# An attention and MLP kernel: the order of the first loads, 21 idle matmuls, and where a weight's high halves are computed

## The chip, the core and the metric

One core of a Trainium2 chip (trn2). The metric is device time of one execution in microseconds (us), as the median of several runs. The engines are TensorE (PE; its weight loads are shown as PEld), VectorE (DVE), ScalarE (ACT), GpSimd (POOL) and SyncE (SP), which issues all DMAs of this kernel.

## What is computed

`x` is 1 x 2048 x 512 in float32. Two branches read the layer-normed `x`; one is a sliding, dilated attention with 32 heads of 16 values, the other an MLP with 1376 hidden units that layer-norms once more.

```python
xn = _layernorm(x, axis=-1)
s = _A_ref(xn, A_wqkv, A_wo)     # q,k,v = xn @ wqkv; each row sees 8 rows, 2 apart, backwards; softmax; @ wo
g = _silu(_B_ref(xn, B_w1, B_b1, B_w2, B_b2))   # gelu(layernorm(xn) @ w1 + b1) @ w2 + b2
return x + s * g
```

## The kernel before

Rows of `x` are split by parity (`c` = 0, 1; the attention goes in steps of two rows) and then into 8 tiles of 128 rows. For a parity the layer-normed tiles are transposed on the PE into `yT`, 512 columns each, and kept there.

**Two halves for each number.** Matmuls run in float16, but every operand is held as a scaled high half and a low half that holds the rest, and each product is made of three: high x high, high x low, low x high. So each weight (`wqkv` in four blocks `hb`, `w1`, `w2`, `wo`) goes through the same steps after its load: ACT sums its squares (`sumsq`, and `prep_q` for `wqkv`), a matmul with the constant tile `fours` adds the sums up over the partitions (`total`, on the PE), a few DVE operations on one column make a power of two from it (`half_exp`, `up`, `down`), then ACT writes the high half (`split`, or `hi` in `prep_q`) and DVE the low half (`lo`, a scalar_tensor_tensor that reads the weight and its high half). `w2` has 11 blocks `k`: the first 8 lie in `yT` tiles, the last 3 in tiles `f`.

**Opening.** `LOADS` sets the order of the first DMAs: `q0` (the first block of `wqkv`, in two parts), then tiles 2 and 3 of `x`, then the other tiles in pairs. `ln0` handles a group of tiles: `stats` (bn_stats and bn_aggr on DVE), `factors` (power -1/2 on POOL, a few DVE columns), the normed tile on DVE or, for the tiles in `ACT_Y`, on ACT (`y_act`), four PE transposes, the high half by ACT, the low half by DVE. `qkv(c, hb, u)` then makes q, k and v of a tile with 12 matmuls of 384 columns, in the order of `IORD`, and ACT writes them to `U`.

**The rest.** `attention` runs on DVE with some additions on POOL. `mlp1(ch, f)` makes 128 hidden units of 512 rows: 12 matmuls of 512 columns, then on ACT the gelu, the high half, and for the first 8 blocks a low half that starts with one more matmul with the diagonal tile `dg`. `mlp2` adds the block into four PSUM tiles. `wo_first` and `wo_last` multiply by `wo`, and DVE and POOL finish the output.

**What sets the order.** All operations are recorded in a plan (`Plan`) with an engine, an estimated duration, what they read and write, and a priority. `Plan.issue` places them one by one: of the operations that could start next on an engine, the one with the smallest priority value within a small window. The program's order on each engine is the result, and each engine then runs its own queue in that order, waiting on semaphores. DMAs are issued by SP in the order of the plan. An operation marked `port` shares a lock in the plan with all others so marked, on DVE and POOL.

## Time and profile before

| | |
|---|---|
| time, median of 3 runs | 425.15 us (423.82 to 425.76) |
| the profiled execution | 426.52 us, its span 424.7 us |
| mean granted TensorE clock | 0.992 |
| busy in the span | PE 406.7 us (96%), DVE 396.7 (93%), ACT 217.6 (51%), POOL 97.8 (23%) |
| costliest group | 768 projection matmuls (L545), 129.3 us busy |
| DMA | 44.83 MB, 106 GB/s on average |

The span runs from the first to the last instruction of the program; the time of an execution has some 1.8 us around it. In the rows of the timeline the columns are the start in us, the duration in us, the engine, the source line and operation, output<-inputs by tile names, the shape, how many instructions were merged, and in brackets how long the engine had been idle and what ended that.

### The profile page before, as it was taken

To read this page: it belongs to the slowest core of one execution; us is meant where nothing else is said; L and a number is where in the kernel's file an instruction comes from. 1 tells how busy PE (TensorE), PEld (TensorE's weight loads), DVE (VectorE), ACT (ScalarE), POOL (GpSimd) and SP (SyncE) were. 2 spreads that over 40 slices of the span, in tenths; PEclk is the share of its full clock that TensorE was granted. 3 is DMA by queue.
4 is the path that set the end of the run, shared out by engine and by line. 5 is a ranking of instruction groups with operands and counts; after the bars stand their busy time and mean duration, and the time that the engine had idled before them with its cause. 6 is when DMAs were issued, how large, how long until landed. Compare 5 with 4: busy or idle time off the path is not lost.

```text
span 424.7 us, 5503 instructions
## 1 busy us (share of the span) xinstructions
PE 406.7 (96%) x2072; PEld 206.6 (49%) x2072; DVE 396.7 (93%) x434; ACT 217.6 (51%) x340; POOL 97.8 (23%) x87
## 2 busy tenths in 40 slices
PE   0999979999999999999999999999999999999995
PEld 0666524445544654445544654455445544444442
DVE  3998999998999979999999999998999999999966
ACT  4799975845376456744466254125312284226400
POOL 5310202002500382002700360046002610250013
PEclk9999969999999999999999999999999999999999
DMA  8964420003241235742162034022423264005325
GB/s 277 412 245 148 146 79 0 2 7 143 85 101 50 100 87 120 129 109 43 54 180 100 0 88 99 2 74 80 155 98 107 69 161 174 0 2 127 122 49 198
DMA packets 43050, 44.83 MB, mean 106 GB/s; under 512 B 27496, under 2 KB 28064, under 8 KB 42768
## 3 DMA queue, kind: packets, MB, share of 16 engines
q1 hardware_dynamic: 43024, 44.49, 34.7%
q8 instruction: 16, 0.26, 0.3%
q14 instruction: 10, 0.08, 0.1%
HBM read 23.53 MB, written 7.34 MB: 73 GB/s over the span
## 4 chain that ended last, share of the span: by engine, by line
PE 84%; ACT 9%; DVE 3%; DMA 2%; issue 1%; SPq 0%; DVEq 0%
PE z L826 27%; PE mh L785 26%; PE ps L545 22%; PE ps L723 6%; ACT w L376 2%; ACT U L553 2%; DMA prod<-in_A_x_dram 2%; ACT w L339 1%; PE z L723 1%; PE mh L723 1%; DVE U L714 1%; DVE U L767 1%; ACT wq L402 1%; ACT yT L495 1%; DVE bn L458 1%
## 5 line engine op out<-in xcount | busy, mean ns | idle before, releaser
L545 PE MATMUL ps<-wq,yT 128*128 128x384 f16 x768 | 129.3, 328 | 0.0
L785 PE MATMUL mh<-yT,w 128*128 128x512 f16 (+1 forms) x528 | 123.5, 385 | 0.9 <-ACT h L813 0.9
L826 PE MATMUL z<-w,h 128*128 128x512 f16 x480 | 112.0, 379 | 0.0
L545 PEld LDWEIGHTS <-yT 128*128 128x128 f16 x768 | 75.5, 99 | 51.1 <-issue 1.5
L785 PEld LDWEIGHTS <-w 128*128 128x128 f16 (+1 forms) x528 | 53.4, 101 | 65.8 <-issue 6.3
L798 ACT ACTIVATE mh<-mh,b1T,hsc 128x512 f32<-128x512 f32 (+1 forms) x44 | 33.0, 749 | 88.0 <-PE mh L785 87.8
L596 DVE TENSOR_TENSOR prod<-U 128x2048 f32<-128x2048 f32 x32 | 74.1, 2317 | 1.0
L826 PEld LDWEIGHTS <-h 128*128 128x128 f16 x480 | 47.1, 98 | 55.3 <-issue 0.3
L599 DVE TENSOR_REDUCE L<-prod 128x128 f32<-128x2048 f32 x32 | 72.9, 2279 | 0.3
L553 ACT ACTIVATE U<-ps,cs 128x384 f32<-128x384 f32 x64 | 37.2, 581 | 67.4 <-PE ps L545 63.4
L653 DVE TENSOR_TENSOR prod<-L,U 128x2048 f32<-128x2048 f32 x28 | 63.4, 2285 | 0.1
L676 POOL COPY gate<-prod 1x1 f32<-1x1 f32 x21 | 4.4, 208 | 210.7 <-DVE prod L596 204.2
L648 DVE TENSOR_TENSOR prod<-prod,prod 128x2048 f32<-128x2048 f32 x16 | 36.5, 2284 | 0.0
L677 POOL TENSOR_TENSOR prod<-prod 128x1024 f32<-128x1024 f32 x14 | 32.9, 2347 | 0.0
L723 PEld LDWEIGHTS <-oT 128*128 128x128 f16 x192 | 18.8, 98 | 22.4
L801 ACT ACTIVATE h<-mh,hsc 128x512 f16<-128x512 f32 x40 | 27.4, 685 | 0.9
L723 PE MATMUL ps<-wo,oT 128*128 128x512 f16 x120 | 26.9, 379 | 0.0
L804 DVE SCALAR_TENSOR_TENSOR h<-mh,hsc,h 128x512 f16<-128x512 f32 x32 | 23.8, 744 | 2.8 <-ACT h L801 2.8
L607 POOL TENSOR_TENSOR L<-L,misc 1x384 f32<-1x384 f32 x8 | 19.4, 2430 | 20.6 <-DVE L L599 20.6
L677 POOL TENSOR_TENSOR prod<-prod,prod 128x1024 f32<-128x1024 f32 x7 | 16.4, 2344 | 0.0
L798 ACT ACT_TABLE_LOAD x12 | 15.4, 1283 | 0.2
L636 ACT ACTIVATE o<-prod,osc 128x1024 f16<-128x1024 f32 (+1 forms) x9 | 9.4, 1050 | 11.5 <-DVE prod L648 6.2
(144 smaller groups left out, 338.1 us busy)
## 6 DMA issues: line engine op xcount, KB each, us to landing
f<-in_A_x_dram SPq DMA_DIRECT2D x31, 256.0 KB, 3.7
U<-U SPq DMA_DIRECT2D x16, 392.0 KB, 3.7
gd<-f SPq DMA_DIRECT2D x12, 256.0 KB, 2.0
oT<-in_B_w_dram SPq DMA_DIRECT2D x2, 1024.0 KB
yT<-in_B_w_dram SPq DMA_DIRECT2D x2, 1024.0 KB
f<-gd SPq DMA_DIRECT2D x8, 256.0 KB, 3.4
out_dram<-f SPq DMA_DIRECT2D x8, 256.0 KB, 2.0
out_dram<-U SPq DMA_DIRECT2D x8, 256.0 KB, 2.3
```

The lines of the kernel that those rows point to most:

```text
L545: nc.tensor.matmul(b.t[:, 0:384], y[:, s, k, o:o + P], wq[:, hb, k, t], start=(n == 0), stop=(n == 11))
L553: act(384, lambda i=i, b=b: nc.scalar.activation(U3[:, i:i + 31:15, :], b.t[:, 0:384].rearrange("p (t e) -> p t e", t=3), AF.Identity, sca ...
L596: dve(2048, lambda p2=p2, g=g: nc.vector.tensor_tensor(p2(), q, slots(Ut, KH, 2 * g), op=ALU.mult), qk + [("kh", ub, 0), ("kh", ub, 1), (" ...
L599: dve(2048, lambda pr=pr, g=g: nc.vector.tensor_reduce(L3()[:, 2 * g:2 * g + 2], pr.t.rearrange("p (r f d) -> p r f d", r=2, d=DH), AX.X, ...
L648: dve(n, lambda: nc.vector.tensor_tensor(d(), a(), b(), op=ALU.add), keys, [dkey])
L653: dve(2048, lambda: nc.vector.tensor_tensor(pr.t.rearrange("p (r f d) -> p r f d", r=2, d=DH), L3()[:, 2 * g:2 * g + 2].rearrange("p r (f ...
L677: nc.gpsimd.tensor_tensor(x.t[:, 0:1024], x.t[:, 0:1024], y(), op=ALU.add)
L723: nc.tensor.matmul(b.t, oT[:, hb, i // 4, s, i % 4], wo[:, hb, t], start=(hb == 0 and n == 0), stop=(hb == NHB - 1 and n == 2))
L785: nc.tensor.matmul(b.t[0:M], w1[:, k, s, f * P:f * P + M], yT[ch][:, t, k], start=(n == 0), stop=(n == 11))
L798: act(512, lambda: nc.scalar.activation(b.t[0:M], b.t[0:M], AF.Gelu_apprx_tanh, bias=b1T[0:M, f:f + 1], scale=hsc[0:M, 1:2]), [b, ("b1T",) ...
L801: act(512, lambda: nc.scalar.activation(hi()[0:M], b.t[0:M], AF.Identity, scale=hsc[0:M, 2:3]), [b], [hk])
L826: nc.tensor.matmul(z.t, hl[s][0:K, t * P:(t + 1) * P], w2[0:K, f, w], start=(f == 0 and n == 0), stop=(f == NF - 1 and n == 2))
```

## The change

The core of the diff (planner constants and the lines that only split a matmul group into smaller pieces are cut):

```diff
-LOADS = ["q0", (2, 1), (3, 1), (0, 2), (4, 2), (6, 2)]
+LOADS = [(2, 1), (3, 1), "q0", "q2", (0, 2), (4, 2), (6, 2)]
...
-                    t, o = min((x for x in lst if x[0] <= t0 + WINDOW), key=lambda x: (x[1].prio, x[1].n))
+                    t, o = min((x for x in lst if x[0] <= t0 + (WINDOW if x[1].prio > PURG else WURG)),
+                               key=lambda x: (x[1].prio, x[1].n))
...
+WAKE = 21
+QHI = 4
...
     def total(dst, dkey, cols, n, ckeys, late=False):
...
+        if n == 2:
+            for k in range(2):
+                pl.add("pe", 0.15, lambda k=k: nc.tensor.matmul(
+                    b.t[:, 0:1], fours, cols()[:, k:k + 1], start=(k == 0), stop=(k == 1)),
+                    [ckeys[k]], [b], prio=min(pl.prio, PTOT))
+            n = 1
...
+    def on_pool(n, hi, src, s, r, w, **k):
+        pool(0.3 + n * POOL1, lambda: nc.gpsimd.tensor_scalar(hi, src(), s, 1.0, op0=ALU.mult, op1=ALU.mult),
+             r, [w], port=False, **k)
...
-    def split(hi, lo, src, s, r, w):
+    def split(hi, lo, src, s, r, w, eng="act"):
...
+        if eng == "pool":
+            on_pool(n, hi, get, s, r, (w, "hi"))
+        else:
+            act(n, lambda: nc.scalar.activation(hi, get(), AF.Identity, scale=s), r, [(w, "hi")])
...
-    IORD = [2, 3, 1, 4, 5, 6, 7, 0]
+    IORD, IORD0 = [2, 3, 1, 4, 5, 6, 7, 0], [2, 3, 0, 1, 4, 5, 6, 7]
...
-            for n0 in range(0, 12, 4) if u < 2 else (0,):
-                n1 = n0 + 4 if u < 2 else 12
+            ends = [1, 2, 3, 4, 8, 12] if u == 0 and i == IORD0[0] else [4, 8, 12] if u < 2 else [12]
+            for n0, n1 in zip([0] + ends, ends):
...
+    idle = fours.bitcast(BF16)
+    for _ in range(WAKE):
+        b = R_mh.new()
+        pl.add("pe", 0.2, lambda b=b: nc.tensor.matmul(b.t[:, 0:2 * P], idle[:, 0:P], idle, start=True,
+                                                       stop=True), [("yd", 2)], [b], prio=1e9)
...
-        sumsq(lambda k=k: cw1.t[:, k:k + 1], (cw1, k), s1a[:, k], ("s1a", k),
+        sumsq(lambda k=k: cw1.t[:, k:k + 1], (cw1, k), s1a[:, k], [("s1a", k)] + [("y_", i) for i in BEFORE_W1],
...
             split(w2[:, k, 0], w2[:, k, 1], (s2a, s2b)[k // 4][:, k % 4], zsc[:, 0:1],
-                  [("s2", k // 4), ("zsc0",), ("w2j", k // 4), ("yT", 2 + k // 4)], ("w2", k))
+                  [("s2", k // 4), ("zsc0",), ("w2j", k // 4), ("yT", 2 + k // 4)], ("w2", k),
+                  "act" if k < 2 else "pool")
         else:
             b = s2c[k - 8]
-            act(512, lambda k=k, K=K, b=b: nc.scalar.activation(
-                w2[0:K, k, 0], b.t[0:K], AF.Identity, scale=zsc[0:K, 0:1]),
-                [b, ("zsc0",), ("w2j", k)], [("w2h", k)])
+            on_pool(512, w2[0:K, k, 0], lambda b=b, K=K: b.t[0:K], zsc[0:K, 0:1],
+                    [b, ("zsc0",), ("w2j", k)], ("w2h", k))
...
+    warm = sb.tile([1, 1], F32, name="warm")
+    act(1, lambda: nc.scalar.activation(warm, ident[0:1, 0:1], AF.Gelu_apprx_tanh),
+        [("y", 0, i) for i in range(NI)] + [("wq", 1, k) for k in range(KT)], [("warm",)], table="gelu")
```

In words: tiles 2 and 3 of `x` are loaded ahead of `q0`; the sum of squares of a `wqkv` block is added up by two matmuls, one for each part, instead of one; the bias column is no longer made for the tiles that DVE norms; ACT's squares of `w1` come after its normed tiles; 21 matmuls of 256 columns on the constant tile `fours`, whose results nobody reads, stand in the PE's queue; nine of the eleven high halves of `w2` (blocks 2 to 10) are written by POOL; an activation on one element loads ACT's gelu table earlier; and the planner weighs priorities in a smaller window, so that the order of the opening changes. `QHI` is 4 and there are four parts, so its branch is never taken.

The first rows of the PE's queue, from the first transposes to the first projections, before (`f_102` and `f_103` are normed tiles, `z` PSUM tiles for transposes and sums, `ps` the projections, `s_128` the columns of sums of the first block of `wqkv`):

```order
L345 MATMUL z_153<-s_128,fours 128x2
L491 MATMUL z_156<-ident,f_102 128x128 x4
L491 MATMUL z_154<-ident,f_103 128x128 x4
L545 LDWEIGHTS yT_88
L545 MATMUL ps_149<-wq,yT_88 128x384
```

And now (`mh_151` and `mh_152` are the PSUM tiles that the idle matmuls write):

```order
L531 MATMUL z_156<-ident,f_102 128x128 x4
L965 LDWEIGHTS fours
L965 MATMUL mh_151<-fours 128x256
L965 LDWEIGHTS fours
L965 MATMUL mh_152<-fours 128x256
L965 LDWEIGHTS fours
L965 MATMUL mh_151<-fours 128x256
L362 MATMUL z_153<-s_128,fours 128x1
```

In one piece, the sums' matmul moves behind the first transposes and three idle matmuls. After these rows come four more idle matmuls, the transposes of the second tile, the second matmul on the sums, fourteen more idle matmuls, and then the projections: everything behind an idle matmul waits for it.

The stretch of ACT's queue that leads to the first gelu, before (`w_85` is `w1` and `w_86` is `w2`, their high halves; `mh` the hidden units in PSUM, `h` their halves, and in the first row a staging tile):

```order
L376 ACTIVATE w_85<-h_113,hsc 128x352
L553 ACTIVATE U_93<-ps_149,cs_120 128x3x128
L376 ACTIVATE w_86<-yT_91,zsc 128x512
L1006 ACTIVATE w_86<-f_106,zsc 128x512
L1006 ACTIVATE w_86<-f_108,zsc 128x512
L1006 ACTIVATE w_86<-f_103,zsc 97x512
L798 ACT_TABLE_LOAD
L798 ACTIVATE mh_151<-mh_151,b1T,hsc 128x512
L402 ACTIVATE wq,s_127<-yT_90 128x2x384
L801 ACTIVATE h_114<-mh_151,hsc 128x512
```

And now:

```order
L405 ACTIVATE w_85<-h_112,hsc 128x352
L593 ACTIVATE U_93<-ps_150,cs_120 128x3x128
L405 ACTIVATE w_85<-h_113,hsc 128x352
L434 ACTIVATE wq,s_127<-yT_90 128x2x384 x2
L841 ACTIVATE mh_152<-mh_152,b1T,hsc 128x512
L844 ACTIVATE h_114<-mh_152,hsc 128x512
L856 ACTIVATE h_114<-mh_152,hsc 128x512
```

The high halves of `w2` and the table load are gone from there, and two squares of the next `wqkv` block stand ahead of the first gelu instead of behind it.

POOL's queue behind the last column operation of the opening, now (before, `hlast` came right behind the column operation):

```order
L490 TENSOR_TENSOR cT<-lw_138,halves 128x2
L396 TENSOR_SCALAR w_86<-yT_90,zsc 128x512 x2
L396 TENSOR_SCALAR w_86<-yT_91,zsc 128x512 x4
L396 TENSOR_SCALAR w_86<-f_103,zsc 128x512
L396 TENSOR_SCALAR w_86<-f_104,zsc 128x512
L396 TENSOR_SCALAR w_86<-f_105,zsc 97x512
L1011 TENSOR_SCALAR hlast<-hlast,hsc 1x512
```

Nine operations on 128 partitions by 512 are new on POOL; the row on `hlast`, on one partition, was there.

More of the change, by code (lines that the diff above doesn't have):

```diff
@@ L387, in tile_mixer, with k0, load_q @@
     stkey = [[xq0], [("U", 1, 2)], [("yT", 2)], [("yT", 3)]]
-    def load_q(hb):
-        pre = pl.users(stkey[hb])
-        for k in range(0, KT, 2):
+    def k0(hb):
+        return dict(rate=400e3, tail=0.6, issue=0.45) if hb == 0 else {}
+    def load_q(hb, kk=range(0, KT, 2)):
+        pre = pl.users([x for x in stkey[hb] if x is not xq0])
+        for k in kk:
             dma(P * 3072, lambda k=k: nc.sync.dma_start(stq[hb]()[:, k * 384:(k + 2) * 384],
                                                         a_wqkv[hb, :, k * 384:(k + 2) * 384]),
-                [], [("stq", hb, k), ("stq", hb, k + 1)] + stkey[hb], after=pre)
+                [], [("stq", hb, k), ("stq", hb, k + 1)] + stkey[hb], after=pre, **k0(hb))
     def prep_q(hb):
@@ L420, in prep_q, with factors @@
             r = [("stq", hb, k), ("qs", hb)]
-            act(384, hi, r, [("wqh", hb, k)], holds=stkey[hb])
+            if hb == 0 and k >= QHI:
+                dve(384, lambda k=k: nc.vector.tensor_scalar(
+                    wq[:, hb, k, 0], stq[hb]()[:, k * 384:(k + 1) * 384], qsc[:, hb, 0:1], None,
+                    op0=ALU.mult), r, [("wqh", hb, k)], holds=stkey[hb], f=0.72)
+            else:
+                act(384, hi, r, [("wqh", hb, k)], holds=stkey[hb])
             dve(384, lo, r + [("wqh", hb, k)], [("wq", hb, k)], holds=stkey[hb], c=0.125,
-                prio=0.135 if hb == 0 else None)
+                prio=PQLO if hb == 0 else None)
         down(qsc[:, hb, 1:2], ("qi", hb), h, 24.0)
     cpos = [2, 3, 0, 1, 4, 5, 6, 7]
-    def factors(n, mv, mk, cdst, ckeys, **k):
+    def factors(n, mv, mk, cdst, ckeys, bias=True, **k):
         A, p0b, rb = R_w.new(), R_w.new(), R_w.new()
@@ L779, in mlp1, with mm @@
         b = R_mh.new()
-        def mm():
-            n = 0
-            for k in range(KT):
-                for (s, t) in ((0, 0), (0, 1), (1, 0)):
-                    nc.tensor.matmul(b.t[0:M], w1[:, k, s, f * P:f * P + M], yT[ch][:, t, k],
-                                     start=(n == 0), stop=(n == 11))
-                    n += 1
-        pe(12, 512, mm, [("y", c, 4 * j + i) for i in range(4)] +
-           [("w1", k, int(f >= 8)) for k in range(KT)], [b])
+        def mm(n0, n1):
+            for n in range(n0, n1):
+                k, (s, t) = n // 3, ((0, 0), (0, 1), (1, 0))[n % 3]
+                nc.tensor.matmul(b.t[0:M], w1[:, k, s, f * P:f * P + M], yT[ch][:, t, k],
+                                 start=(n == 0), stop=(n == 11))
+        for n0 in range(0, 12, 3) if ch == 0 and f < 3 else (0,):
+            n1 = n0 + 3 if ch == 0 and f < 3 else 12
+            pe(n1 - n0, 512, lambda n0=n0, n1=n1: mm(n0, n1),
+               [("y", c, 4 * j + i) for i in range(4)] +
+               [("w1", k, int(f >= 8)) for k in range(n0 // 3, n1 // 3)], [b],
+               after=pl.users([b]))
         if f < NF - 1:
```

57 lines of the change are left out of this document (33 added, 24 removed).

## The prediction

> **What bounds the kernel now.** I read the page first, then the timeline of the opening and of the first MLP blocks, then the waits.
>
> ```profile
> PE   0999979999999999999999999999999999999995
> PE 84%; ACT 9%; DVE 3%; DMA 2%; issue 1%; SPq 0%; DVEq 0%
> ```
>
> The PE is busy in all 40 slices but the first, the sixth and the last, and it is 84% of the chain that ended last. So a microsecond counts if it brings the PE's stream forward or closes a hole in it. There are two such places. The first is the opening.
>
> ```profile
> 3.94 0.84 ACT L402 ACTIVATE wq<-prod 128x768 bf16<-128x768 f32 x1 [1.94 <-DMA prod<-in_A_wqkv_dram]
> 4.43 0.52 POOL L961 MEMSET hlast<- 1x512 f16 x1
> 5.96 0.70 DVE L458 BATCH_NORM_STATS2 bn<-prod 128x6 f32<-128x512 f32 x1 [4.96 <-DMA prod<-in_A_x_dram]
> 6.06 0.19 ACT L402 ACTIVATION_READ_ACCUMULATOR wq<-prod 128x1 f32 x1
> 6.30 0.59 PE L345 MATMUL z<-s,fours 128*128 128x2 f32 x2 [6.30 <-ACT wq L402]
> 6.94 0.69 DVE L458 BATCH_NORM_STATS2 bn<-prod 128x6 f32<-128x512 f32 x1
> 8.38 2.13 ACT L413 ACTIVATE wq<-prod,qsc 128x384 f16<-128x384 f32 x4 [2.13 <-DVE qsc L369]
> 9.27 1.29 DVE L458 BATCH_NORM_STATS2 bn<-prod 128x6 f32<-128x512 f32 x2 [0.79 <-DMA prod<-in_A_x_dram]
> 10.53 0.54 DVE L484 TENSOR_SCALAR f<-prod,lw,lw 128x512 f32<-128x512 f32 x1
> 11.22 1.94 PE L491 MATMUL z<-ident,f 128*128 128x128 f32 x8 [4.33 <-DVE f L484]
> 12.34 0.59 ACT L495 CAST yT<-z 128x512 f16<-128x512 f32 x1 [1.83 <-PE z L491]
> 12.98 3.39 PE L545 MATMUL ps<-wq,yT 128*128 128x384 f16 x12
> 14.49 1.14 DVE L417 SCALAR_TENSOR_TENSOR wq<-prod,qsc,wq 128x384 f16<-128x384 f32 x2
> 16.20 1.04 PE L491 MATMUL z<-ident,f 128*128 128x128 f32 x8
> 17.08 4.06 PE L545 MATMUL ps<-wq,yT 128*128 128x384 f16 x24
> 24.82 9.91 PE L545 MATMUL ps<-wq,yT 128*128 128x384 f16 x60
> ```
>
> The weights' high halves are done at 10.51 (8.38 + 2.13), but the first projection starts at 12.98. The `x` path is late: tile 2 lands at 5.96, and DVE then stands at 9.27 in the statistics of the next pair, so the normed tile 2 begins only at 10.53. The twelve first projections take 0.28 us each, later ones 0.165 (9.91/60), and the same eight transposes 1.94 and then 1.04: the PE's clock is low at first. At 17.08 the PE has done 12 projections and 8 transposes, at later prices 12 x 0.165 + 1.04 = 3.0 us. Its stream thus stands as if it had run at full price since **14.1**.
>
> The second place is a hole at the first MLP blocks.
>
> ```profile
> 48.78 5.34 PE L785 MATMUL mh<-yT,w 128*128 128x512 f16 x24
> 50.72 1.96 ACT L1006 ACTIVATE w<-f,zsc 128x512 f16<-128x512 f32 x3
> 52.70 1.28 ACT L798 ACT_TABLE_LOAD   x1
> 54.00 0.75 ACT L798 ACTIVATE mh<-mh,b1T,hsc 128x512 f32<-128x512 f32 x1
> 56.23 0.38 PE L810 MATMUL mh<-h,dg 128*128 128x512 f16 x1 [2.10 <-ACT h L801]
> 57.47 5.28 PE L785 MATMUL mh<-yT,w 128*128 128x512 f16 x12 [0.87 <-ACT h L813]
> 62.55 0.43 PE L345 MATMUL ps<-s,fours 128*128 128x2 f32 x2
> 57.00:63.00 6.00, 5.53 (x15) 2.35 (x15) 6.00 (x4) 3.68 (x9) 0.00 (x0) 0.50 0.01 4
> 66.40 2.59 PE mh L785 x12
> ```
>
> Two blocks fill both `mh` tiles by 54.12; ACT is still at high halves of `w2` and its table load, and gives the first gelu at 54.00. The PE waits 2.1 and 0.9 us, and meanwhile its clock falls: in the stretch from 57 to 63 (the last column but two is the granted clock) it is 0.50, and a block takes 5.28 us instead of 2.59. From 54.12 to 62.55 are 8.43 us for one block and one matmul with `dg`, 2.59 + 0.22. The hole costs **5.6 us**: 2.9 waiting, 2.7 slow clock.
>
> **The change part by part.** *The opening.* By order of bytes, tile 2 (256 KB instead of 384 KB first) lands before 3.94, about 3.4. The second part of `q0` is now fourth, as tile 3 was, so about 6.9. Its statistics (0.7) and two short column operations are then done before POOL's memsets end at 4.95, so the power starts there (0.55, as in a row below, at 15.77), and the normed tile (0.54) is done at about 6.1. Four transposes at the low clock (12.34 - 11.22) give 7.3, ACT's high half 7.9. It stands ahead of the second square in ACT's queue, so that square and its read end near 8.9, where before it was 6.25. From there to the first high half were 2.13 us; now a PE matmul that stands behind tile 3's transposes and a low half and a bn_stats on DVE (0.7 each) lie between its steps, so I take 3: 11.9. The four high halves come at 0.53 each, until 14.0; the first projection is split so that it follows them. Four low halves of 0.57 and three bn_stats on DVE end near 16.4, when 20 projections are done, worth 20 x 0.165 = 3.3 us: the stream stands at 13.1 instead of 14.1. **-1.0 us**, +-1.
>
> The idle matmuls cost 21 x 0.22 = 4.6 us at the low clock (half of 5.28/12), between 7.3 and 11.9. The transposes of tile 3 and the sums stand behind them, which is in the 3 us above; the rest lies in the wait for the high halves and costs nothing. If the high halves came early, what is left over would stand on the path.
>
> They are to raise the clock before the first projection. TensorE's page in the Trainium skill (TensorE: Matmul & The Clock Gate, Part 1) says that the clock rises after a busy, free-running window of about 3.4 us, whose phase is not the program's; by that the idle run can just miss it. No run here shows that phase. If the clock is low at the first projections, they cost 12 x (0.28 - 0.165) = 1.4 us as before; the sum has it up by 12.5.
>
> *The hole.* Nine high halves leave ACT, four take 2.56 (the row below, at 37.57) and three 1.96, so 0.60 each, 5.4 us; the table load is only earlier on the same queue, and two squares (0.84 and a read of 0.19 each, which overlap: about 0.95) come ahead of the first gelu: 5.4 - 1.9 = 3.5 us earlier, 50.5. The first block is ready at 51.4 (48.78 + 2.6), so the gelu no longer waits for ACT, and no square stands between it and the high half: gelu and high half, 0.75 us each or less, take 1.5 us, less than the second block's 2.6. The hole goes: **-5.6 us**.
>
> *What is late next.* DVE's low halves of `w1`, which the first block needs to its last part.
>
> ```profile
> 37.57 2.56 ACT L376 ACTIVATE w<-yT,zsc 128x512 f16<-128x512 f32 x4
> 15.77 0.55 POOL L452 TENSOR_TENSOR cT<-lw,halves 128x1 f32<-128x1 f32 x1 [2.36 <-DVE lw L447]
> 43.39 1.28 DVE L377 SCALAR_TENSOR_TENSOR w<-oT,hsc,w 128x1024 f16<-128x1024 f32 x1
> 43.60 2.52 POOL L962 TENSOR_SCALAR hlast<-hlast,hsc 1x512 f16<-1x512 f16 x1 [18.21 <-DVE hsc L369]
> 44.65 0.65 DVE L952 TENSOR_SCALAR dg<-ident,hsc 128x128 bf16<-128x128 f32 x1
> 45.23 3.66 DVE L377 SCALAR_TENSOR_TENSOR w<-oT,hsc,w 128x1024 f16<-128x1024 f32 x3
> 376.76 1.08 POOL L607 TENSOR_TENSOR L<-L,misc 1x384 f32<-1x384 f32 x1 [0.38 <-DVE L L599]
> 376.79 3.21 DVE L596 TENSOR_TENSOR prod<-U 128x2048 f32<-128x2048 f32 x1
> L596 DVE TENSOR_TENSOR prod<-U 128x2048 f32<-128x2048 f32 x32 | 74.1, 2317 | 1.0
> 419.14 1.26 POOL L716 TENSOR_TENSOR U<-U,f 128x512 f32<-128x512 f32 x1 [2.49 <-DVE U L767]
> ```
>
> Before, the fourth low half ends at 48.89 (45.23 + 3.66) and is needed by the twelfth matmul, at 51.2: 2.3 us of room. Now one more low half of `w2` (0.7) stands ahead of it, and the PE comes up to 1 us sooner: about 1 us of room is left. Into this stretch the nine POOL operations fall, about seven of them between DVE's low halves of `w2` and `w1`. Do they hold DVE up? The nearest row is POOL's own tensor_scalar L962: while it runs, from 43.60 to 46.12, two of the same low halves (L377) go at full speed, 1.28 and 1.22 us; only L952 takes 0.65 us where its 128 columns would want some 0.2 by L484 (0.54 for 512). So 0 to 0.45 us for each. Seven times that, less 1 us of room, is 0 to +2.2; I take the middle, **+1.1**.
>
> A POOL operation of this size lasts at most 1.26 by its nearest row of that shape (L716, two inputs): nine in 11 us from about 37, done by 48, which hides them. If each took 2.52 like L962, the fourth would end at 47.1; in DVE's queue three low halves of `w1` stand behind its low half, 47.1 + 0.7 + 3 x 1.22 = 51.5 for a block that wants them at 50.2: +1.3, inside the range.
>
> *Does it reach the end?* DVE is 93% busy and its low halves do not get earlier.
>
> ```profile
> DVE U L767 <- PE ps L723: 3.2, 1, 3.2
> DVE h L804 <- ACT h L801: 2.8, 3, 2.1
> DVE f L516 <- ACT f L515: 2.5, 1, 2.5
> ```
>
> At the end DVE waits 3.2 us for the PE; 2.8 and 2.5 it waits for ACT results that themselves follow the PE's matmuls or late tiles. That is 8.5 us, more than the gain, so the PE still ends last. The rest (two matmuls for the sums, no bias column, `QHI` never taken) is some tenths in both directions, taken as nothing.
>
> **Sum:** -1.0 - 5.6 + 1.1 = -5.5 us. The profiled execution of 426.52 (span 424.7) becomes 421.0. It lay 1.4 us over the median of the runs, 425.15, which becomes **419.7**.
>
> **The rivals.** *Slower: POOL locks DVE out.* The rows at 376.76 and 376.79 speak for it: POOL's L607 starts first, and a DVE operation with two inputs in SBUF takes 3.21 instead of 2.32, 0.9 us more, as long as the POOL operation. If each of the seven holds DVE for 0.9 to 1.26 us, the first block stands for 5.3 to 7.8 us, and the clock falls as at 57 (+2.7): -6.6 + 8.0 to 10.5 = +1.4 to +3.9, **427.8**. It decides from 0.7 us a piece. Against it: L607 reads two tiles, and L962, a tensor_scalar, let L377 pass. The Trainium skill (SBUF — State Buffer, Who interferes with whom) says that a VectorE instruction with two SBUF inputs and a GpSimd one that reads SBUF exclude each other for the whole instruction. By that rule this rival would hold; the rows at 376 agree, L962 beside L377 does not.
>
> *A partial hold that costs the clock.* 0.45 us a piece, a stall of 2.2 us like the 2.1 of before, and the block at half clock: -6.6 + 2.2 + 2.7 = -1.7, 423.4.
>
> *DVE becomes the bound.* If only the 3.2 us at the end are real slack, the gain stops there: -3.2, **421.9**.
>
> *The opening does not do what it says.* The clock is low when the projections start, or `q0`, now third, lands late: +1 instead of -1.0, so -3.5, **421.6**.
>
> **How the numbers follow.** Forecast 0.60, around 419.7, from 417.5 (no hold, opening 1 us better) to 421.5. POOL locks DVE out 0.13. Partial hold with the clock lost 0.09. DVE the bound 0.09. Opening 0.09. The range takes in all but the lock-out and half a microsecond of spread: 417.0 to 424.2. Half a percent, 2.1 us, is about what a measurement of this kernel can tell from no change: faster is below 423.0, slower above 427.3. Faster: 0.60 + 0.09 + 0.09 and a quarter of the partial hold, 0.80. Slower: most of the lock-out, 0.11. Same: 0.09.
>
> **What would show it.** Right: the first projections at 0.165 us each and from about 12.5; L841 following the first MLP block with no PE idle over 0.5 us and a clock of 1.00 from 50 to 65; L406 on `w1` at 1.22 to 1.28. Wrong: L406 or L636 lengthened beside L396 on POOL, PE idle before L824 with DVE named as releaser, a clock of 0.50 after 50, or a wait of the PE on `oT` near the end.

## The result and the profile after

The changed kernel takes **425.89 us** (median of 20 runs, 425.22 to 426.99); the kernel before, on the same chip, 425.39 (20 runs, 423.79 to 427.45). The ratio is 1.0015, with a 95% interval of 1.0004 to 1.0026: no change that matters, if anything a little slower. The forecast was 419.7, and the measured time lies outside its range. The profiled execution after took 425.66 us, its span is 423.9, 0.8 us shorter than the span before.

From the page of the kernel after, the PE's busy tenths and the engines' shares of the chain that ended last:

```profile
PE   3999999999999999999999999999999999999995
PE 76%; DVE 12%; ACT 6%; DMA 4%; issue 2%; SPq 1%; DVEq 0%
```

The hole in the sixth slice is gone. But the PE's share of the chain fell from 84% to 76%, and DVE's rose from 3% to 12%: a stretch of the run now waits for DVE.

**The opening.** The timeline of the kernel after:

```profile
9.52 0.19 ACT L434 ACTIVATION_READ_ACCUMULATOR wq<-prod 128x1 f32 x1
10.56 0.43 PE L362 MATMUL z<-s,fours 128*128 128x1 f32 x2
10.85 2.37 PE L965 MATMUL mh<-fours 128*128 128x256 bf16 x14
11.02 0.16 DVE L373 TENSOR_SCALAR ssq<-z 128x1 f32<-128x1 f32 x1 [1.17 <-PE z L362]
12.93 2.13 ACT L445 ACTIVATE wq<-prod,qsc 128x384 f16<-128x384 f32 x4 [1.54 <-DVE qsc L391]
13.59 0.32 PE L585 MATMUL ps<-wq,yT 128*128 128x384 f16 x1 [0.38 <-ACT wq L445]
15.11 2.92 PE L585 MATMUL ps<-wq,yT 128*128 128x384 f16 x17 [0.18 <-ACT wq L445]
```

The second square of `q0` is read at 9.71, the first high half starts at 12.93 (forecast 11.9), and 20 projections are done at 18.0 (forecast 16.4).

**The first MLP blocks.** The PE's timeline after:

```profile
54.04 0.39 PE L824 MATMUL mh<-yT,w 128*128 128x512 f16 x1 [0.38 <-DVE w L406]
56.48 0.38 PE L853 MATMUL mh<-h,dg 128*128 128x512 f16 x1
56.70 3.04 PE L824 MATMUL mh<-yT,w 128*128 128x512 f16 x12
59.58 0.38 PE L853 MATMUL mh<-h,dg 128*128 128x512 f16 x1
```

And a window over the stretch (the last column but two is the granted clock):

```profile
55.00:63.00 8.00, 7.87 (x38) 3.58 (x38) 8.00 (x9) 5.97 (x11) 0.00 (x0) 1.00 0.40 106
```

No wait for ACT shows in these rows, and the clock stays at 1.00. The small wait that is left is for DVE's low halves (L406).

**A ledger of the PE's lost time.** All kernels here have the same useful matmuls. At the full clock's pitch (0.2158 us for 512 columns, 0.1625 for 384, 0.109 for a transpose) they are worth 399.33 us. A matmul's start, less the price of all useful matmuls ahead of it, is the time that the PE has lost by then. The table splits it at equal amounts of work done: 10 us of work (the opening, to about 24 us), 38 (to the first MLP blocks), 55 (past the hole), 95 and 150, and the end. Each row is one profiled execution; the experiments in it are told below.

| us lost by the PE | opening | to 38 | hole | to 95 | to 150 | rest | sum |
|---|---|---|---|---|---|---|---|
| before | 13.39 | 0.71 | 6.45 | 0.19 | 0.01 | 0.05 | 20.8 |
| after | 14.33 | 2.94 | 0.56 | 1.92 | 0.01 | 0.18 | 19.9 |
| e1, w2 half alone | 14.34 | 1.12 | 1.90 | 2.50 | 1.80 | 0.18 | 21.8 |
| e2, opening alone | 14.60 | 0.97 | 6.69 | 0.18 | 0.01 | 1.33 | 23.8 |
| e3, early table load alone | 14.84 | 0.81 | 4.51 | 0.19 | 0.43 | 0.19 | 21.0 |
| e4, after, no idle matmuls | 13.54 | 2.81 | 0.56 | 2.84 | 0.01 | 0.72 | 20.5 |
| e7, after, GpSimd twice | 13.73 | 3.99 | 0.56 | 3.69 | 0.01 | 0.18 | 22.2 |
| e9, after, half pairs | 13.85 | 2.93 | 0.56 | 0.19 | 0.01 | 0.05 | 17.6 |
| e10, before, half pairs | 13.51 | 0.72 | 4.92 | 0.19 | 0.01 | 0.06 | 19.4 |
| e11, after, 5 blocks on GpSimd | 14.56 | 1.40 | 2.38 | 0.95 | 0.01 | 0.38 | 19.7 |
| e16, after, 3 blocks on GpSimd | 14.17 | 1.40 | 2.97 | 0.97 | 0.75 | 0.24 | 20.5 |
| e15, before, 1 block on GpSimd | 13.41 | 1.07 | 1.94 | 0.14 | 1.60 | 0.17 | 18.3 |

So in the two traces the hole gave 5.9 us, as forecast. The opening took 0.9 back, the way to the first MLP blocks 2.2, and the stretch behind the hole 1.7.

On the way to the first MLP blocks the changed kernel's PE waits at three places, two of them here, the third in the row at 54.04 above. PE and ACT after:

```profile
41.69 0.35 PE L367 MATMUL z<-s,fours 128*128 128x1 f32 x2 [0.53 <-DVE s L371]
49.07 1.14 PE L585 MATMUL ps<-wq,yT 128*128 128x384 f16 x6 [0.43 <-ACT U L593]
44.86 1.15 ACT L405 ACTIVATE w<-oT,hsc 128x1024 f16<-128x1024 f32 x1 [1.47 <-DVE hsc L386]
```

By the ledger's count these places lose 0.9, 0.6 and 0.5 us of the 2.9. The first and the last wait for DVE; at 49.07 the PE waits for ACT, which had itself waited 1.47 us for DVE.

**Where DVE is late.** The change leaves DVE's work nearly as it was, but DVE comes later to the same place. The first product with the softmax weights, before:

```profile
79.46 6.69 DVE L653 TENSOR_TENSOR prod<-L,U 128x2048 f32<-128x2048 f32 x3
```

and after, with nearly the same instructions ahead of it:

```profile
84.20 6.69 DVE L693 TENSOR_TENSOR prod<-L,U 128x2048 f32<-128x2048 f32 x3
```

That is 4.7 us later, while the PE is 2.7 us earlier at 55 us of work (lost time 17.8 instead of 20.5). Up to there DVE was busy 74.4 us instead of 70.6; the other 1.0 us is idle time. Of the 3.8 us of busy time, 2.8 are in nine instructions that run beside GpSimd's pieces, and 0.7 is one more `bn_stats` that the new order has ahead. (A piece is one of the nine high halves.) The timeline after, GpSimd and DVE:

```profile
38.63 0.69 POOL L396 TENSOR_SCALAR w<-yT,zsc 128x512 f16<-128x512 f32 x1
39.30 2.73 POOL L396 TENSOR_SCALAR w<-yT,zsc 128x512 f16<-128x512 f32 x1
42.01 1.12 POOL L396 TENSOR_SCALAR w<-yT,zsc 128x512 f16<-128x512 f32 x1
38.77 2.70 DVE L636 TENSOR_TENSOR prod<-U 128x2048 f32<-128x2048 f32 x1 [0.84 <-DMA U<-U]
41.47 1.10 DVE L406 SCALAR_TENSOR_TENSOR w<-yT,zsc,w 128x512 f16<-128x512 f32 x1
44.81 0.52 DVE L992 SCALAR_TENSOR_TENSOR s<-s,s 128x1 f32<-128x1 f32 x1
47.02 1.64 DVE L406 SCALAR_TENSOR_TENSOR w<-oT,hsc,w 128x1024 f16<-128x1024 f32 x1
```

The two take turns. The piece at 39.30 begins while DVE's product runs and ends at 42.03, 0.56 us after it. The low half at 41.47 then takes 0.36 us more than its 0.74, and the next piece, at 42.01, ends 0.56 us after that low half. So five of the eight low halves of `w2` take 1.03 to 1.11 us, the first of `w1` 1.64 instead of 1.27, a product 2.70 instead of 2.28, and an operation on one column 0.52 instead of 0.15. The groups by shape (count | busy us, mean ns | idle before) before:

```profile
L377 DVE SCALAR_TENSOR_TENSOR w<-yT,zsc,w 128x512 f16<-128x512 f32 x8 | 5.8, 744 | 0.0
```

and after:

```profile
L406 DVE SCALAR_TENSOR_TENSOR w<-yT,zsc,w 128x512 f16<-128x512 f32 x8 | 7.5, 947 | 0.0
```

Not all of the 4.7 us comes from GpSimd: e2 below, which has the new opening and no piece on GpSimd, starts this product at 81.69. By these single traces some 2.2 us come with the opening and its order and 2.5 with the `w2` half.

What the late DVE costs is seen some 30 us further on. The timeline after, ACT and PE:

```profile
76.35 0.62 ACT L445 ACTIVATE wq<-yT,qsc 128x384 f16<-128x384 f32 x1 [1.79 <-DVE qsc L386]
77.17 1.28 ACT L663 ACT_TABLE_LOAD   x1
79.31 1.28 ACT L841 ACT_TABLE_LOAD   x1
80.60 0.75 ACT L841 ACTIVATE mh<-mh,b1T,hsc 128x512 f32<-128x512 f32 x1
85.61 0.68 ACT L844 ACTIVATE h<-mh,hsc 128x512 f16<-128x512 f32 x1
82.51 0.38 PE L853 MATMUL mh<-h,dg 128*128 128x512 f16 x1 [0.26 <-ACT h L844]
86.34 0.38 PE L853 MATMUL mh<-h,dg 128*128 128x512 f16 x1 [0.87 <-ACT h L844]
```

ACT's queue has a high half of the next `wqkv` block, which waits 1.79 us for a column operation that stands behind the logits in DVE's queue, and the exp of the first softmax, which needs these logits, ahead of the gelu of the next block; and each change of function loads a table (1.28 us). Before, the first of these loads stood 4.6 us earlier, and the PE did not wait:

```profile
72.58 1.28 ACT L623 ACT_TABLE_LOAD   x1
```

Now the PE is ahead, and it waits twice.

### The profile page after: what moved, and what is told of

The parts are those of the page before. It is cut to its first block, busy times and chain, and to the rows that moved or that the text cites. A ratio compares the mean times of both kernels' runs of the same rounds, so it can differ in the third digit from the quotient of the medians.

```text
span 423.9 us, 5554 instructions
## 1 busy us (share of the span) xinstructions
PE 409.1 (97%) x2101; PEld 208.3 (49%) x2101; DVE 400.7 (95%) x427; ACT 213.7 (50%) x332; POOL 106.0 (25%) x96
## 4 chain that ended last, share of the span: by engine, by line
PE 76%; DVE 12%; ACT 6%; DMA 4%; issue 2%; SPq 1%; DVEq 0%
PE z L869 23%; PE ps L585 21%; PE mh L824 21%; PE ps L763 6%; DVE prod L636 3%; PE z L763 2%; DVE L L639 2%; DVE prod L693 2%; DVE w L406 2%; DMA prod<-in_A_wqkv_dram 1%; DMA yT<-in_A_wo_dram 1%; PE mh L763 1%; ACT U L593 1%; ACT w L405 1%; DVE prod L688 1%
## 5 line engine op out<-in xcount | busy, mean ns | idle before, releaser
L824 PE MATMUL mh<-yT,w 128*128 128x512 f16 (+1 forms) x528 | 121.9, 379 | 0.5 <-DVE w L406 0.4
L636 DVE TENSOR_TENSOR prod<-U 128x2048 f32<-128x2048 f32 x32 | 74.4, 2326 | 1.8 <-DMA U<-U 0.8
L717 POOL TENSOR_TENSOR prod<-prod,prod 128x1024 f32<-128x1024 f32 x7 | 16.4, 2343 | 0.0
L480 POOL TENSOR_TENSOR lw<-lw,halves 128x2 f32<-128x2 f32 (+2 forms) x6 | 5.1, 852 | 36.5 <-DVE lw L482 28.3
```

Of the source, the lines that this page charges most:

```text
L636: dve(2048, lambda p2=p2, g=g: nc.vector.tensor_tensor(p2(), q, slots(Ut, KH, 2 * g), op=ALU.mult), qk + [("kh", ub, 0), ("kh", ub, 1), (" ...
L717: nc.gpsimd.tensor_tensor(x.t[:, 0:1024], x.t[:, 0:1024], y(), op=ALU.add)
L824: nc.tensor.matmul(b.t[0:M], w1[:, k, s, f * P:f * P + M], yT[ch][:, t, k], start=(n == 0), stop=(n == 11))
```

## The experiments

Each kernel is compared with the kernel before on its own chip. "After" and "before" in a diff tell which of the two kernels was edited. In e7, e9 and e10 the order of every engine is that of the edited kernel, and in e4 nearly so. All other edits make the planner place much of the program anew, so their times hold the effect of another order too.

### The halves of the change

**e1**, on the kernel before: `on_pool` and the `eng` argument of `split` added, and

```diff
-                  [("s2", k // 4), ("zsc0",), ("w2j", k // 4), ("yT", 2 + k // 4)], ("w2", k))
+                  [("s2", k // 4), ("zsc0",), ("w2j", k // 4), ("yT", 2 + k // 4)], ("w2", k),
+                  "act" if k < 2 else "pool")
...
+    act(1, lambda: nc.scalar.activation(warm, ident[0:1, 0:1], AF.Gelu_apprx_tanh),
...
```

with blocks 8 to 10 on `on_pool` too. 

> The kernel before with the w2 half of the change alone: high halves of blocks 2 to 10 on GpSimd and the early gelu table load, opening untouched. Theory (the opening takes 3.2 us away, the w2 half brings 6.4 - 0.6 at the first MLP blocks, of which a DVE that is late between 62 and 100 us takes back 1.5 to 2.5): 421.4 to 423.0, and PE idle or late again between 75 and 100 us. Rival (GpSimd holds DVE so long that nothing of it reaches the end): 425 or above. Rival (nothing is taken back): 419.7 to 420.5.

Measured 427.10 us, ratio 1.0046 (1.0028 to 1.0064). The w2 half alone is slower, in the range of the first rival. The ledger has both sums: the hole shrinks to 1.9, but 2.5 us are lost up to 95, more than in the changed kernel, and another 1.8 near 155, which the theory did not have.

**e2**, on the kernel after: all eleven high halves back on ACT, no early table load. This half also holds the planner's new estimates, priorities and a tie rule. They make the new order, and not a smaller window: the window is 0.05 us in both kernels. 

> The changed kernel with all of w2's high halves back on ACT and no early table load: the opening half alone. Theory (the opening loses 3.2 us up to the first MLP blocks, and the hole there stays): 428 to 429. Rival (the loss is hidden, since the first MLP blocks wait for ACT at the same time as before): 425 to 426. Rival (the opening is worth the 1.0 us that was forecast): 424.4.

Measured 429.41, ratio 1.0102 (1.0083 to 1.0122). The opening alone is 4.3 us slower. Its direction was as the theory said, but not its place: up to the first MLP blocks it lost only 15.6 us, like kernels with the old opening (14.1 to 15.7). The hole costs as much as in the profiled execution before (6.7), but in another way: there is one stretch of 3.4 us at half clock instead of two, and the PE waits longer. The PE of e2:

```profile
58.83 0.38 PE L853 MATMUL mh<-h,dg 128*128 128x512 f16 x1 [3.22 <-ACT h L844]
```

That wait was 2.10 before. ACT's table load for the gelu ends at 56.7 here and at 54.0 before, so the new opening makes ACT late too. Another 1.3 us are lost near 283 and 319. The clock of the four runs was 0.990 to 0.993, where the kernel before is mostly at 0.995; in the trace a part of that is the last 2.3 us of the span, behind the PE's work, where 0.50 is granted.

**e3**, on the kernel before: the early table load alone. 

> The kernel before with the early gelu table load alone, w2 untouched on ACT. If the 1.3 us load stands in the row that PE waits for, its move is worth up to 1.3: 424.1. If ACT has work without a gap until the hole, the load only changes its place and the time stays at 425.4, or rises by up to 1.3 where it now stands ahead of evictions.

Measured 423.44, ratio 0.9975 (0.9957 to 0.9993): faster by 1.6 us, more than the load lasts (the order of the rest is new too). Nine of its 12 runs had a clock of 0.998 or more and took 423.4 on average, three had 0.995 and took 426.1. This led to the clock, next.

**e4**, on the kernel after: `WAKE = 0`. 

> The changed kernel without its 21 idle matmuls. Theory (they bring the granted clock up before the first projections, which else run at 0.32 instead of 0.165 us for about 4 us): 1.0 to 1.7 us slower than the changed kernel, 426.9 to 427.6. Rival (the first projections wait for ACT's and DVE's halves anyway): 425.9, with the clock step some 4 us later in the trace.

Measured 426.57, ratio 1.0039 (1.0023 to 1.0054), against 1.0015 (1.0004 to 1.0026) with the idle matmuls. The full clock is granted from 16.1 us on instead of 12.3; over all traces it comes at 9.9 to 15.4 us with idle matmuls and at 15.6 to 17.7 without. The intervals just overlap, so their worth, 0.7 to 1.0 us, is likely but not certain. Where it comes from is not shown: e4's opening lost 13.54 us, less than the changed kernel's 14.33, but its `q0` landed 1.8 us earlier, and what e4 loses more is behind the hole. That they cost nothing is supported.

### The clock in the hole

The kernel before ran 100 times beside these experiments. Its mean clock has three values: 0.992 (11 runs, 426.5 us on average), 0.995 (57 runs, 425.5) and 0.997 or more (32 runs, 424.1). Traces show what they are. In the profiled execution before (0.992) the PE ran at half clock from 56.5 to 63.4, 6.8 us; in the trace of e10 below, which has the same hole and a clock of 0.995, only half as long. The windows of e10:

```profile
57.00:60.00 3.00, 2.39 (x6) 0.84 (x6) 3.00 (x3) 3.00 (x7) 0.00 (x0) 0.50 0.00 1
57.00:63.00 6.00, 5.39 (x22) 2.51 (x22) 6.00 (x6) 4.85 (x11) 0.00 (x0) 0.72 0.00 1
```

Its PE's timeline:

```profile
57.61 4.11 PE L790 MATMUL mh<-yT,w 128*128 128x512 f16 x12 [0.87 <-ACT h L818]
```

The block that took 5.28 us in the profiled execution takes 4.11 here, with the same waits of 2.1 and 0.9 ahead of it. So the hole holds none, one or two stretches of 3.4 us at half clock. In the traces one costs 1.5 us and two 2.7; by the averages of the runs one costs 1.4, and two cost 2.4. (The third group is read from the mean clock alone; no trace caught a run of this kernel without a stretch.) The 2.7 that the prediction took was the rarest of the three, and the median run has one stretch.

**e15**, on the kernel before: the early table load, and block 10 alone on GpSimd. 

> The kernel before with the early table load and block 10 alone on GpSimd. Theory (the early load shortened PE's wait enough that the clock mostly stays up; one piece of 0.65 us less on ACT shortens it further, and holds DVE 0.4): 422.7 to 423.4, all runs at clock 0.998 or more. Rival (another order later in the run eats it, as with three pieces): 424.5 to 425.

Measured 424.45, ratio 0.9977 (0.9965 to 0.9990), and all 12 runs at 0.997 or more. The trace of e15 has a wait of 0.48 us instead of 2.10 for the first gelu, the same 0.87 for the second, and a second block at full clock:

```profile
54.98 0.38 PE L818 MATMUL mh<-h,dg 128*128 128x512 f16 x1 [0.48 <-ACT h L809]
56.23 2.75 PE L793 MATMUL mh<-yT,w 128*128 128x512 f16 x12 [0.87 <-ACT h L821]
```

The clock is as the theory said, but the time missed its 422.7 to 423.4 and lies at the rival's, since 1.6 us are lost near 155 as in e1. With e3 it is the best version found here: e3 0.9975, e15 0.9977 of the time before, both some 0.4% under the changed kernel's ratio.

### Is DVE the bound behind the hole?

**e5** on the kernel after and **e6** on the kernel before:

```diff
+            if u == 0 and n == 3:
+                dve(128, lambda g=g: nc.vector.memset(L3()[:, 2 * g:2 * g + 2], 0.0), [], [(L, g)])
+                continue
```

> The changed kernel, with the fourth pair of products and sums of the first attention unit replaced by one memset: leaves out a quarter of that unit's logits, 4.3 us of DVE's work near 70 us. Theory (DVE reaches the first exp 4.7 us late, and the table loads that follow it hold up the first-layer evictions at 82 and 86 us): the 1.45 and 0.47 us that PE loses there come back, 423.8 to 424.4, no PE wait of L844 near 82 and 86. Rival (the lost time is PE's and ACT's own): 425.9.

> The kernel before with the same pair replaced by a memset (a quarter of the first unit's logits left out). Theory (DVE is not the bound there before the change; it waits 2.1 us for ACT at 97): 425.1 to 425.4, no change. Rival (any DVE work of 4.3 us less is worth 1 us or more in both kernels): 424.4 or less.

Measured 426.57 (ratio 1.0039, 1.0023 to 1.0054) and 426.87 (1.0031, 1.0009 to 1.0053): both got slower with less work. These two don't answer the question. The planner placed everything behind the edit anew; in e6 1.8 us are lost near 231 that were not there before, and in e5 1.2 us of PE waits for gelus come earlier, with another loss of 1.0 near 202. An edit that changes the plan is two edits.

**e9** on the kernel after and **e10** on the kernel before repeat the question with the plan's cost of 2048 elements left in, so that each engine's order stays as it was but for the memsets:

```diff
+            r1 = 1 if u == 0 and n > 1 else 2
-            dve(2048, lambda p2=p2, g=g: nc.vector.tensor_tensor(p2(), q, slots(Ut, KH, 2 * g),
-                                                                op=ALU.mult),
+            dve(2048, lambda p2=p2, g=g, r1=r1: nc.vector.tensor_tensor(
+                p2()[:, 0:r1], q[:, 0:r1], slots(Ut, KH, 2 * g)[:, 0:r1], op=ALU.mult),
...
+                if r1 == 1:
+                    nc.vector.memset(L3()[:, 2 * g + 1:2 * g + 2], 0.0)
```

> The changed kernel with the order of every engine kept, but the third and fourth pair of products and sums of the first attention unit done on half of their elements (the other half of those logits is set to zero): about 4.2 us of DVE's work less before its first maximum at 75 us. Theory (DVE, held by GpSimd, comes 4.7 us later to this point than before the change, and what PE loses between 75 and 105 us follows from that): 1.4 to 1.9 us back, 424.0 to 424.5. Rival (PE's loss there is ACT's two table loads, whatever DVE does): 425.9.

> The same edit in the kernel before, order kept. Theory (PE is the bound there and DVE has to spare): 425.1 to 425.4. Rival (DVE sets the pace of both kernels): 424.0 or less.

Measured 424.23 (ratio 0.9977, 0.9960 to 0.9993) and 425.16 (0.9995, 0.9975 to 1.0014), against 1.0015 and 1 without the edit. The same work taken off DVE brings the changed kernel 1.6 us and the kernel before nothing that can be told from zero. The rival falls: with DVE in time the two table loads are still there, but 2.4 us earlier, and the PE does not wait. ACT's timeline in e9:

```profile
74.78 1.28 ACT L668 ACT_TABLE_LOAD   x1
76.91 1.28 ACT L846 ACT_TABLE_LOAD   x1
```

The window over its MLP blocks, with the PE busy throughout:

```profile
80.00:100.00 20.00, 20.00 (x98) 9.40 (x96) 20.00 (x18) 10.57 (x19) 0.00 (x0) 1.00 0.09 26
```

And the engines' shares of its chain:

```profile
PE 88%; ACT 5%; DVE 2%; DMA 2%; issue 1%; SPq 0%; DVEq 0%
```

DVE's share of the chain goes from 12% to 2%, and the loss between 55 and 95 us of work from 1.92 to 0.19. That DVE is the bound there after the change, and was not before, is shown.

### What a GpSimd piece costs

**e7**, on the kernel after, each high half of `on_pool` written twice by the same recorded operation, the order of all else kept:

```diff
-        pool(0.3 + n * POOL1, lambda: nc.gpsimd.tensor_scalar(hi, src(), s, 1.0, op0=ALU.mult, op1=ALU.mult),
-             r, [w], port=False, **k)
+        def twice():
+            for _ in range(2):
+                nc.gpsimd.tensor_scalar(hi, src(), s, 1.0, op0=ALU.mult, op1=ALU.mult)
+        pool(0.3 + n * POOL1, twice, r, [w], port=False, **k)
```

> The changed kernel with each of the nine high halves on GpSimd written twice, same order of all else. Theory (each 1.23 us piece holds DVE's instructions beside it 0.35 to 0.45 us, and DVE is late from there to 100 us): DVE 3 to 4 us later at the first exp, time 427.5 to 429.5. Rival (GpSimd costs DVE nothing that reaches the end): 425.9 to 426.4.

Measured 429.12, ratio 1.0094 (1.0068 to 1.0120): 3.2 us more than the changed kernel for nine more pieces. In the ledger 1.05 us of it lie on the way to the first MLP blocks and 1.77 behind the hole. DVE reaches the first exp 2.2 us later (the table load at 79.37 instead of 77.17), not 3 to 4 as expected; its instructions beside GpSimd take 4.9 us more than usual, 2.2 more than in the changed kernel. The pieces reach into other low halves now; the groups of e7:

```profile
L408 DVE SCALAR_TENSOR_TENSOR w<-yT,zsc,w 128x512 f16<-128x512 f32 x8 | 7.5, 952 | 0.5 <-POOL w L398 0.5
L408 DVE SCALAR_TENSOR_TENSOR w<-o,hsc,w 128x352 f16<-128x352 f32 x2 | 1.9, 1008 | 0.0
```

The 352-column half takes 1.01 us instead of 0.57, and the 1024-column one 1.56 on average instead of 1.27. (In e7 DVE also waits 0.5 us for the second writing.)

**e11** and **e16**, on the kernel after: `"act" if k < 6` in the place of `k < 2`, five pieces; and only blocks 8 to 10, three pieces. 

> The changed kernel with only blocks 6 to 10 of w2 on GpSimd, 0 to 5 on ACT: five pieces instead of nine. By the lost time per piece (about 0.4 us each, over nine) the four pieces off GpSimd give DVE 1.6 us back, and ACT takes 2.6 us more ahead of the first MLP blocks. If ACT has that room: 424.5 to 425.3. If the wait at the first MLP blocks comes back in part: 426 to 428.

> The changed kernel with only blocks 8 to 10 on GpSimd. By 0.4 us a piece DVE gets 2.4 us back against nine pieces and 0.8 against five; ACT has 1.3 us more than with five. If ACT's wait at the first MLP blocks grows by no more than what DVE gets back: 423.6 to 424.4. If it grows by the whole 1.3 us and the clock falls: 425.5 to 427.

Measured 424.40 (ratio 0.9987, 0.9973 to 1.0001) and 426.23 (1.0024, 1.0009 to 1.0039). With 0 (e2, which also lacks the early table load), 3, 5, 9 and 18 pieces under the new opening the times stand at 1.0102, 1.0024, 0.9987, 1.0015 and 1.0094 of the time before: the best is in the middle, where what comes back at the first MLP blocks and what DVE loses balance (the hole costs 2.97, 2.38 and 0.56 with 3, 5 and 9 pieces, the stretch behind it 0.97, 0.95 and 1.92). In e16 the clock falls in 5 of 12 runs.

**e8** and **e12**, on the kernel before: the early table load and blocks 8 to 10 on GpSimd; e12 adds to the first gated sum of the second unit a dependence on the second normalization's power, which so comes ahead of it:

```diff
-                    pool(2.45, fn, [acc, p3, pr], [x, ("gate",)], prio=p)
+                    pool(2.45, fn, [acc, p3, pr] + ([("c", 1, 0)] if u == 1 else []), [x, ("gate",)], prio=p)
```

> The kernel before with the early gelu table load and only blocks 8 to 10 of w2 on GpSimd. Theory (3 pieces take 1.9 us off ACT ahead of the first MLP blocks and hold DVE 1.2 us, less than the 2.1 us it has): 421.5 to 423.0, better than the early load alone (423.4). Rival (any piece on GpSimd costs more than it brings): 423.9 to 425.5.

> The kernel before with the early table load and three blocks on GpSimd, as in the earlier run, and the second normalization's power (3.6 us on GpSimd near 152) placed ahead of the gated sum that stood before it. Theory (PE lost 1.9 us at 155 because ACT's evictions waited for that power behind a 2.5 us piece): 422.7 to 423.5. Rival (PE, now ahead, is held there by DVE's own place, whatever GpSimd's order): 424.5 to 425.

Measured 424.95 (ratio 1.0003, 0.9987 to 1.0018) and 427.00 (1.0045, 1.0027 to 1.0063). In e8 the hole is down to 1.8 us, a gain of 3.1 to 4.7, and 2.3 are lost again between 95 and 150. ACT in e8:

```profile
156.13 0.68 ACT L537 ACTIVATE cs<-cT,qsc 128x8 f32<-128x8 f32 x3 [3.85 <-POOL cT L460]
```

and in e12:

```profile
152.86 0.88 ACT L537 ACTIVATE cs<-cT,qsc 128x8 f32<-128x8 f32 x4 [3.50 <-POOL cT L460]
```

With the power first on GpSimd ACT still waits 3.5 us for it, and the PE still loses 1.8: it is DVE's columns that the power waits for, so the rival holds. A PE that comes 2 to 3 us earlier meets DVE's place there. That the time of e12 is still 2 us above e8's comes from another order at the end: 6.4 us lie between the end of the PE's work and the end of its span, about 4.6 in all traces here but three.

**e14**, on the kernel after with five pieces: `port=True` in `on_pool`. 

> The changed kernel with blocks 6 to 10 on GpSimd and the planner told that a GpSimd piece and a DVE instruction can't run side by side (its port flag), so that its order reckons with the hold. If the loss comes from an order that was made without the hold: 422.5 to 424. If the hold itself is the price, whatever the order: 424.4 as with the five pieces before, or above.

Measured 427.79, ratio 1.0056 (1.0037 to 1.0075). It has the long end of 6.4 us too (1.8 of the 3.4 us above e11), so its time does not settle whether an order that knows of the hold would be better. Its order does keep the two apart: DVE's instructions beside pieces take 0.06 us more than usual, 1.3 in e11. But DVE starts the first product with the softmax weights at 87.80, the latest of all traces, and between the opening and 150 us of work e14 loses 5.0 us, e11 4.7: nothing speaks for it.

**e13**, on the kernel after: `LOADS = ["q0", "q2", (2, 1), (3, 1), (0, 2), (4, 2), (6, 2)]`. 

> The changed kernel with the loads in the old order: both halves of the head block's weights first, then the x tiles; the rest of the opening kept. Theory (the opening is worth nothing: the first high half needs the weights, which land 3 us later behind the x tiles): 425.0 to 425.9, first projection at or before that of the changed kernel (13.6 us). Rival (the x tiles first are what the reordered opening lives on): 426.5 to 427.5.

Measured 427.49, ratio 1.0048 (1.0031 to 1.0065). The PE of e13 in the opening:

```profile
10.40 1.16 PE L585 MATMUL ps<-wq,yT 128*128 128x384 f16 x3
15.04 0.82 PE L965 MATMUL mh<-fours 128*128 128x256 bf16 x6
18.80 1.36 PE L531 MATMUL z<-ident,f 128*128 128x128 f32 x8 [0.88 <-ACT f L500]
```

The first projection starts 3.2 us earlier than in the changed kernel, as the theory wanted, but idle matmuls now stand among the projections and the next transposes come late: 15.33 us are lost in the opening, and 17.1 up to the hole against the changed kernel's 17.3. It is the third trace with the long end, whose 1.8 us cover the whole difference in time. So the old order of the loads is shown neither better nor worse.

## Why the prediction was wrong, step by step

**The hole, -5.6: right.** Its cause (ACT's high halves and table load), its end and its price in that trace held: -5.9 in the ledger, clock 1.00 throughout.

**From the profiled execution to the median: wrong by 1.4.** The sum took the whole 2.7 us of slow clock away and then subtracted 1.4 because the profiled execution lay above the median. That excess was the slow clock: its second stretch. The median run had only 1.4 of it to lose. With the same -5.5 the median should have been put at 421.0, not at 419.7.

**The opening, -1.0: wrong.** `q0` landed later than taken (ACT's first square on it starts at 7.46, where the second part had been put at 6.9, and the second square ended at 9.71, not 8.9). The way from there to the first high half took 3.2 us instead of 3, and the 20 projections were done 5.1 us behind its start instead of 4.5. The clock was not the reason: it is full from 12.3 on, ahead of the first projection, as the sum had it. The trace gives +0.9. The step behind it failed too: one trace cannot tell 1 us there. Over eight traces each, the old opening lost 13.39 to 14.84 us (mean 13.95), the new one 13.58 to 14.60 (mean 14.16): no gain, and a loss of 0.2 that this spread does not resolve.

**The idle matmuls at 0: right**, perhaps better than that (e4).

**DVE's low halves, +1.1: wrong in mechanism and in place.** The sum took half of a hold of 0 to 0.45 us for seven pieces, less 1 us of room, because L962 had let L377 pass. That row was misread. L962's 2.52 us are themselves a wait: in 16 of 18 traces this operation ends 1.44 to 1.46 us after the end of the low half that it started beside. Behind that low half DVE had L952, with one input in SBUF, and only then the next low half; that this gave L962 its turn is likely, and not shown. In e1 a low half comes next, and it takes 1.01 us where 0.57 is usual, although the GpSimd operation is on one partition:

```profile
50.20 1.72 POOL L970 TENSOR_SCALAR hlast<-hlast,hsc 1x512 f16<-1x512 f16 x1
50.40 1.01 DVE L385 SCALAR_TENSOR_TENSOR w<-h,hsc,w 128x352 f16<-128x352 f32 x1
```

What the nine pieces held up in the changed kernel was eight DVE instructions, 0.29 to 0.42 us each, 2.8 us in all. The PE lost 0.5 us of it at the low half at 54.04; the rest made DVE late for what stands behind. The Trainium skill (SBUF — State Buffer, Who interferes with whom) says that the two exclude each other for the whole instruction. The traces agree that they exclude each other: a piece is held until DVE's instruction ends. DVE is held for less than the 0.69 us that a piece takes alone. So the rival that POOL locks DVE out had the mechanism right, and the forecast had it at 0.13. Its price, 0.9 to 1.26 us a piece, was too high: the first block waited 0.4 us for DVE and not 5.3 to 7.8, and the clock stayed up. That its time (427.8) is nearer to the measured one is in part luck.

**"Does it reach the end?": wrong, 1.7 us.** DVE's 8.5 us of waits were counted over the whole run. What counts is DVE's slack up to the next place where the PE, through ACT, needs it. The windows of the kernel before (busy time of PE, PEld and DVE after the length) show what there was:

```profile
40.00:60.00 20.00, 17.03 (x87) 8.55 (x86) 20.00 (x33) 19.97 (x34) 2.52 (x1) 0.91 0.41 131
60.00:80.00 20.00, 20.00 (x89) 9.30 (x88) 19.93 (x28) 11.56 (x19) 3.05 (x1) 0.92 0.00 1
```

DVE was idle for 0.07 us in 40, so what GpSimd took from it came through to the first exp. What that costs the PE is shown by e9: with 4.2 us of DVE's work taken away the loss there goes from 1.92 to 0.19. The rival "DVE becomes the bound" named the engine, but put its place at the end.

Together, in the two traces: opening +1.9 against the forecast, the way to the first MLP blocks and the stretch behind the hole 4.0 lost instead of 1.1, hole 0.3 better, the rest 0.1: 4.6 of the 4.7 us between -5.5 and -0.8. With 1.4 from the median that is 6.0 of the 6.2 us of the miss.

**What stays open.** Why the same waits bring one stretch at half clock in some executions and two or none in others. How DVE's 4.7 us split: the holds (2.8), one more `bn_stats` (0.7) and idle time (1.0) are counted in one trace, and e2 has 2.2 of the 4.7 without a piece. How much of the 2.2 us before the first MLP blocks is GpSimd's hold: neither half alone loses it (e1 1.12, e2 0.97, together 2.94), twice the pieces lose 1.05 more. High halves on GpSimd placed beside DVE instructions that are not held, with the rest of the order as it was, were not tried.

## What to carry to other kernels

Before a stall is priced by one profile, look at how the clock and the time vary over the runs: a stretch at half clock that comes in some executions only is worth its mean, and an execution above the median may be above it for the very thing that the change removes. When the second engine is over 90% busy, count its slack only up to the next place where the bound engine needs it, and price work on GpSimd as time of DVE too. When one row seems to show that two engines pass each other, look at how long both rows took, and at what stood behind them. When a planner makes the order, test a cost with an edit that leaves the order alone; otherwise new losses of 1 to 2 us elsewhere hide the answer.

## What the hardware showed that was not expected

**GpSimd and a DVE instruction with two inputs in SBUF take turns.** Thirteen traces hold 92 pieces. 28 of them find no such instruction running, and take 0.69 to 0.70 us. The other 64 take 0.84 to 2.81 us, and every one ends 0.47 to 0.57 us after the end of the DVE instruction that ran when it began, or that started up to 0.05 us after it. One in e11, GpSimd and DVE:

```profile
39.54 2.72 POOL L396 TENSOR_SCALAR w<-f,zsc 128x512 f16<-128x512 f32 x1
39.09 2.60 DVE L636 TENSOR_TENSOR prod<-U 128x2048 f32<-128x2048 f32 x1 [0.93 <-DMA U<-U]
```

The other way round, a DVE instruction that is held takes 0.27 to 0.47 us more, about the same for one column (0.36) as for 2048 (0.30 to 0.47). Sums with one input are not held: before, 21 of the 32 sums of 2048 columns (L599) run beside a GpSimd addition of 1024 columns, and take 2.25 to 2.29 us as the other eleven do.

**Half clock comes in units of 3.4 us**: two of them in one trace and one in two others, behind the same waits of the PE (2.1 and 0.9 us); and by the mean clock none in the 12 runs of e15, whose trace has a first wait of 0.5.
